# Part of the output stores issued by GpSimd, w_in loaded in three pieces, and the order table rearranged, in an attention and gated-convolution kernel on one core

## The chip, the cores and the metric

The kernel runs on one core of one Trainium2 chip. The metric is the time of one execution on the device, in microseconds (us). A run is called fast or slow by its agreement with the other runs of the same kernel, and only fast runs are compared. The engines are named as the profile names them: PE (matrix products), PEld (the loading of PE's weights), DVE (VectorE), ACT (ScalarE), POOL (GpSimd), SP (SyncE, which issues most DMAs). A profile has durations in ns where it gives the mean of one instruction, and in us elsewhere. The granted clock is the share of PE's full clock that the trace records as granted; where a trace has no clock record for a stretch, the views print 1.00.

## The reference, cut to what matters

```python
# q, k, v: [8 batches, 8 heads, 576, 64]; window of 32 to each side
scores = scale * q @ k^T
scores = where(|i - j| <= 32, scores, -1e9)
attn   = softmax(scores)
x      = (attn @ v) brought to [8, 576, 512]
# feed-forward part, d_ff = 1024, a convolution of 3 taps along the sequence
h      = relu(x @ w_in)
conv   = sum over k of conv_w[k] * h shifted by k - 1
out    = (h * sigmoid(conv)) @ w_out
```

## The kernel before

The kernel first makes a list of named operations (a cast, a product, a mask, a tap of the convolution, a store) and then emits them in the order of a long table. An entry such as `1047G1` reads: operation 1047, on GpSimd, with buffer 1. The letters are P (PE), V (VectorE), S (ScalarE), G (GpSimd), D (a DMA by SyncE), Q (a DMA issued by ScalarE); `2F` is two fillers, matmuls of a zero tile whose result nobody reads. Every engine works through its own entries in this order.

```python
BUFS = {'st': 3, 'qkb': 5, 'qkT': 3, 'attn': 2, 'rec': 4, 'xn': 3, 'hT0': 8, 'hT1': 6, 'hT2': 6, 'cp': 2, 'gT': 4, 'y': 7}
...
# a copy or cast on the engine that the table names
if e in loader:  loader[e].dma_start(out_, in_)
elif e == "S":   scalar.copy(out=out_, in_=in_)
elif e == "V":   vector.tensor_copy(out=out_, in_=in_)
else:            gpsimd.tensor_scalar(out=out_, in0=in_, scalar1=1.0, scalar2=0.0, op0=ALU.mult, op1=ALU.add)
...
# V shifted by half a block, for the odd blocks of queries
copy(e, vo[0:64, c0:c1], ve[64:128, c0:c1])
copy(e, vo[64:128, c0:c1], ve[0:64, c0 + 1:c1 + 1])
...
# the window's mask, after the exponential: both operands in SBUF
(vector if e_ == "V" else gpsimd).tensor_tensor(out=attn, in0=attn, in1=mask, op=ALU.mult)
...
# the convolution of one unit (128 channels x 384 positions); h is hT, in SBUF, pc is in PSUM
gpsimd.tensor_scalar(out=cp, in0=taps(kk), scalar1=w_tap(kk), scalar2=0.0, ...)      # a product on GpSimd
gpsimd.tensor_tensor(out=cp0, in0=cp0, in1=cp1, op=ALU.add)                          # their sum
tensor.matmul(pc, diag_w[:, kk, m, :], taps(kk), ...)                                # a tap on PE
vector.scalar_tensor_tensor(out=pc, in0=taps(kk), scalar=w_tap(kk), in1=from_, op0=ALU.mult, op1=ALU.add)
#   from_ is pc (PSUM) after taps on PE, or cp (SBUF) where GpSimd made the rest: a "lone tap"
vector.tensor_tensor(out=pc, in0=pc, in1=cp0, op=ALU.add)                            # PE's and GpSimd's parts
...
# stores: the table has D, SyncE, for all 36
loader[e_].dma_start(out_rows[r0:r0 + 128, :], y_sb.ap)
```

The gate, the eviction of q and k, xn and y read one operand from PSUM. The mask and the lone tap have two operands in SBUF. The casts and the shifts of V copy from SBUF to SBUF.

The softmax here doesn't subtract the row's maximum and nothing guards it: scores larger than these inputs give would overflow.

## Time and profile before

Before: 227.27 us, median of 3 runs (227.18 to 227.44). The profiled execution spans 225.6 us.

| engine | busy us | share of the span |
|---|---|---|
| PE | 211.5, of which 13.5 are fillers | 94% |
| VectorE | 197.3 | 87% |
| ScalarE | 187.5 | 83% |
| GpSimd | 137.7 | 61% |

The lines that carry the reading of the bound stand in the prediction. The following ones, from the groups of instructions of VectorE and GpSimd kept apart by shape, are the rows that the rest of this document is about. The columns are the source line, the engine, the operation, output and inputs, shapes and types, the count, then the busy time in us and the mean of one in ns, then the idle time before them and what ended it.

```profile
L232 DVE SCALAR_TENSOR_TENSOR gT<-pf,hT 128x384 bf16<-128x384 f32 x88 | 46.8, 548 | 5.4 <-ACT pf L232 5.1
...
L232 DVE TENSOR_TENSOR attn<-attn,mask 128x1152 bf16<-128x1152 bf16 x26 | 23.0, 886 | 2.4 <-ACT attn L232 2.3
L232 DVE SCALAR_TENSOR_TENSOR pf<-hT,conv_w_sb,cp 128x384 f32<-128x384 bf16 x33 | 20.4, 630 | 0.0
...
L232 DVE COPY vo<-ve 64x520 bf16<-64x520 bf16 x10 | 4.1, 410 | 0.7 <-ACT ve L232 0.5
```

```profile
L232 POOL TENSOR_TENSOR attn<-attn,mask 128x1152 bf16<-128x1152 bf16 x6 | 14.2, 2371 | 8.4 <-ACT attn L232 8.4
```

The gate reads PSUM and SBUF and takes 548 ns. The lone tap is of the same size, reads two tiles in SBUF, and takes 630 ns. The mask on GpSimd takes 2.4 us, more than two and a half times as long as on VectorE.

### The profile page before, as it was taken

To read this page: it belongs to the slowest core of one execution; us is meant where nothing else is said; L and a number is where in the kernel's file an instruction comes from. 1 tells how busy PE (TensorE), PEld (TensorE's weight loads), DVE (VectorE), ACT (ScalarE), POOL (GpSimd) and SP (SyncE) were. 2 spreads that over 40 slices of the span, in tenths; PEclk is the share of its full clock that TensorE was granted. 3 is DMA by queue.
4 is the path that set the end of the run, shared out by engine and by line. 5 is a ranking of instruction groups with operands and counts; after the bars stand their busy time and mean duration, and the time that the engine had idled before them with its cause. 6 is when DMAs were issued, how large, how long until landed. Compare 5 with 4: busy or idle time off the path is not lost.

```text
span 225.6 us, 7189 instructions
## 1 busy us (share of the span) xinstructions
PE 211.5 (94%) x2720; PEld 122.9 (54%) x2720; DVE 197.3 (87%) x467; ACT 187.5 (83%) x474; POOL 137.7 (61%) x203
## 2 busy tenths in 40 slices
PE   7698899989989999989999998999999999999993
PEld 5366567658555655545555454545655565455541
DVE  6279869899999979797999788989999999899990
ACT  2689899998989889879889989689989999777642
POOL 5978654654376937695368736756386735566640
PEclk9889999999999999999999999999999999999999
DMA  6999999999989999999997989994535212501224
GB/s 201 331 285 358 355 266 281 321 308 253 290 170 324 317 175 287 236 306 224 288 347 129 202 278 358 182 231 147 144 36 118 99 46 49 175 1 49 93 101 178
DMA packets 66391, 48.16 MB, mean 214 GB/s; under 512 B 50781, under 2 KB 50805, under 8 KB 66357
## 3 DMA queue, kind: packets, MB, share of 16 engines
q1 hardware_dynamic: 64992, 46.32, 78.6%
q10 hardware_dynamic: 1364, 1.39, 2.9%
q8 instruction: 21, 0.34, 0.8%
q14 instruction: 14, 0.11, 0.2%
HBM read 32.52 MB, written 9.44 MB: 186 GB/s over the span
## 4 chain that ended last, share of the span: by engine, by line
PE 41%; DVE 18%; ACT 17%; DMA 13%; issue 5%; SPq 3%; POOL 2%; DVEq 0%; ACTq 0%; POOLq 0%
PE pf L232 41%; DMA st<-in_k_dram 7%; ACT attn L232 6%; DVE pf L232 5%; DVE gT L232 4%; SPq L232 3%; DMA out_dram<-y 3%; ACT xn L232 3%; DVE qkT L232 2%; ACT pf L232 2%; DMA vo<-ve 2%; DVE attn L232 2%; DVE xn L232 2%; ACT qkb L232 2%; ACT y L232 1%
## 5 line engine op out<-in xcount | busy, mean ns | idle before, releaser
L232 PE MATMUL pf<-xT,w_in_sb 128*128 128x385 bf16 (+2 forms) x416 | 73.4, 315 | 3.6 <-ACT hT L232 0.9
L232 PE MATMUL pf<-w_out_sb,gT 128*128 128x512 bf16 x288 | 72.2, 380 | 0.0
L232 POOL TENSOR_SCALAR cp<-hT,conv_w_sb 128x384 f32<-128x384 bf16 (+1 forms) x63 | 38.9, 622 | 46.1 <-ACT hT L232 20.2
L232 ACT ACTIVATE pf<-pf 128x384 f32<-128x384 f32 (+1 forms) x104 | 48.2, 477 | 13.1 <-DVE pf L232 11.1
L232 DVE SCALAR_TENSOR_TENSOR gT<-pf,hT 128x384 bf16<-128x384 f32 (+1 forms) x104 | 52.1, 517 | 5.5 <-ACT pf L232 5.1
L232 PEld LDWEIGHTS <-w_in_sb 128*128 128x128 bf16 x416 | 38.6, 98 | 27.8 <-issue 4.5
L232 ACT ACTIVATE attn<-pf 128x512 bf16<-128x512 f32 (+1 forms) x96 | 41.4, 522 | 1.8 <-PE pf L232 1.8
L232 ACT ACTIVATE hT<-pf 128x385 bf16<-128x385 f32 (+2 forms) x76 | 35.4, 487 | 6.0 <-PE pf L232 5.6
L232 PEld LDWEIGHTS <-gT 128*128 128x128 bf16 x288 | 26.0, 98 | 25.7 <-DVE gT L232 0.5
L232 DVE SCALAR_TENSOR_TENSOR pf<-hT,conv_w_sb,pf 128x384 f32<-128x384 bf16 (+1 forms) x61 | 34.7, 586 | 1.2 <-PE pf L232 1.1
L232 PE MATMUL pf<-hT,diag_w 128*128 128x384 bf16 (+1 forms) x153 | 30.9, 309 | 0.9 <-DVE xn L232 0.6
L232 POOL TENSOR_SCALAR qkb<-st 128x1152 bf16<-128x1152 f32 (+1 forms) x23 | 25.7, 1122 | 7.6 <-DMA st<-in_k_dram 3.2
L232 DVE COPY qkT<-pf 128x576 bf16<-128x576 bf16 x35 | 25.6, 750 | 4.9 <-PE pf L232 4.9
L232 POOL TENSOR_TENSOR cp<-cp,cp 128x384 f32<-128x384 f32 (+1 forms) x24 | 24.4, 1016 | 1.6
L232 DVE TENSOR_TENSOR attn<-attn,mask 128x1152 bf16<-128x1152 bf16 x26 | 23.0, 886 | 2.4 <-ACT attn L232 2.3
L232 ACT ACTIVATE xn<-pf,rec 128x64 bf16<-128x64 f32 x96 | 22.0, 360 | 1.5 <-DVE rec L232 1.5
L232 ACT COPY y<-pf 128x512 f32<-128x512 f32 x30 | 18.1, 605 | 3.9 <-PE pf L232 3.7
L232 DVE SCALAR_TENSOR_TENSOR pf<-hT,conv_w_sb,cp 128x384 f32<-128x384 bf16 (+1 forms) x35 | 21.2, 618 | 0.0
L232 POOL TENSOR_TENSOR attn<-attn,mask 128x1152 bf16<-128x1152 bf16 x6 | 14.2, 2371 | 8.4 <-ACT attn L232 8.4
L232 DVE TENSOR_TENSOR xn<-pf,rec 128x256 bf16<-128x256 f32 x48 | 18.9, 410 | 0.0
L232 ACT COPY qkT<-pf 128x576 bf16<-128x576 bf16 x29 | 18.6, 664 | 0.4 <-PE pf L232 0.2
L232 PEld LDWEIGHTS <-diag_w 128*128 128x128 bf16 x153 | 13.3, 97 | 9.8 <-issue 1.3
(49 smaller groups left out, 235.2 us busy)
## 6 DMA issues: line engine op xcount, KB each, us to landing
st<-in_q_dram SPq DMA_DIRECT2D x16, 576.0 KB, 6.8
out_dram<-y SPq DMA_DIRECT2D x36, 256.0 KB, 3.8
st<-in_k_dram SPq DMA_DIRECT2D x14, 576.0 KB, 8.2
vst<-in_v_dram SPq DMA_DIRECT2D x24, 256.0 KB, 7.0
vst<-in_v_dram SPq DMA_DIRECT2D x15, 192.0 KB, 5.7
vo<-ve SPq DMA_DIRECT2D x11, 260.0 KB, 5.6
st<-in_moe_w_in_dram SPq DMA_DIRECT2D x2, 1024.0 KB, 9.3
st<-in_moe_w_out_dram SPq DMA_DIRECT2D x2, 1024.0 KB, 9.4
```

The source lines that it names most:

```text
L232: return lambda *args, **kwargs: fixed(do(*args, **kwargs))
```

## The change

The words that came with the change name the stores, w_in and the order. The diff holds more. Part of it, with cuts:

```diff
-BUFS = {'st': 3, 'qkb': 5, 'qkT': 3, 'attn': 2, 'rec': 4, 'xn': 3, 'hT0': 8, 'hT1': 6, 'hT2': 6, 'cp': 2, 'gT': 4, 'y': 7}
+BUFS = {'st': 4, 'qkb': 5, 'qkT': 3, 'attn': 2, 'rec': 7, 'xn': 2, 'hT0': 5, 'hT1': 8, 'hT2': 7, 'cp': 6, 'gT': 3, 'y': 5}
+MASKS = ('aa', 'mm', 'mm', 'mm', 'mm', 'mm', 'mm', 'mm')
 CONV = (
-    '33333333',
-    '33q3323r23223321',
+    '32r233q3',
+    'q2233r3q322q3321',
 ... (ten more rows; q, r: taps on GpSimd and a lone tap on VectorE)
 ORDER = """ ... every entry is new ... """
+    W_PARTS = {"in": ((0, 2), (2, 4), (4, MB)), "out": ((0, MB // 2), (MB // 2, MB))}
 ...
+                if added:      # the mask as a product on PE, ahead of the exponential: batch 0 only
+                    for n, e, width in ((2, x, 2), (0, 0, 8), (1, 1, 8)):
+                        tensor.matmul(ps[n]..., outside[rows, :], ident[rows, None, rows]..., start=True, stop=False)
 ...
-            loader[e_].dma_start(out_rows[r0:r0 + 128, :], y_sb.ap)
+            (gpsimd if e_ == "G" else loader[e_]).dma_start(out_rows[r0:r0 + 128, :], y_sb.ap)
```

Counted in the two built programs, from before to after: fillers 75 to 5; GpSimd's products for the convolution 63 to 78 and their sums 24 to 32; lone taps on VectorE 35 to 43; VectorE's taps on PSUM 61 to 38; VectorE's masks 26 to 19, GpSimd's 6 to 9, and batch 0's four on PE; q/k evictions on VectorE 35 to 24; shifts of V on VectorE 10 to 16 (nine of them of double width, which are two shifts in one instruction), on GpSimd 7 to 16, by DMA 11 to 8; stores by SyncE 36 to 21, by GpSimd 0 to 15. What it does in sum: work leaves ScalarE and VectorE for GpSimd, which had 39% of its time free.

## The prediction

> **What bounds the kernel now.** I read the page first, its busy shares and its chain of waits.
>
> ```profile
> PE 211.5 (94%) x2720; PEld 122.9 (54%) x2720; DVE 197.3 (87%) x467; ACT 187.5 (83%) x474; POOL 137.7 (61%) x203
> PE 41%; DVE 18%; ACT 17%; DMA 13%; issue 5%; SPq 3%; POOL 2%; DVEq 0%; ACTq 0%; POOLq 0%
> ```
>
> Three engines are nearly full and GpSimd (POOL) has room. The chain goes through PE, DVE and ACT in turn, so no single one is "the" bound. PE's 94% flatters it: ends of matmuls are modelled, and part of the work is not work. The list of groups kept apart by form shows the fillers, matmuls of zeros that only keep PE running:
>
> ```profile
> L232 PE MATMUL pf<-zero 128*128 128x256 bf16 x75 | 13.5, 330 | 1.3 <-DVE zero L232 1.3
> ```
>
> Without them PE has 211.5 - 13.5 = 198 us of busy time. Next, the table of busy time in four stretches that I chose: the head (until the first FFN matmul), the part in which attention and loads run beside the FFN, the dense part, and the end.
>
> ```profile
> core 0: us, PE busy (x) PEld busy (x) DVE busy (x) ACT busy (x) POOL busy (x), PEclk, DMA share, GB/s
> 0.00:26.00 26.00, 21.33 (x331) 14.66 (x332) 17.63 (x57) 18.73 (x46) 19.87 (x65) 0.93 0.98 299
> 26.00:136.00 110.00, 105.20 (x1560) 63.08 (x1559) 98.42 (x236) 99.09 (x253) 67.31 (x76) 1.00 1.08 267
> 136.00:191.00 55.00, 54.75 (x676) 30.14 (x676) 53.68 (x124) 48.73 (x131) 34.45 (x41) 1.00 0.58 139
> 191.00:226.00 35.00, 30.22 (x157) 15.03 (x155) 27.52 (x54) 20.97 (x46) 16.09 (x22) 0.98 0.28 98
> ```
>
> In the head PE is busy for 21.3 us, of which the same table for the zero tile alone gives 13.5 to the fillers: some 8 us of real work in 26. From 26 to 136, DVE and ACT each are busy for about 90%. From 136 to 191 DVE has 53.7 of 55 us: there PE and DVE are both full. The timeline tells where the head ends and what it waited for, and that ACT then ran without a break:
>
> ```profile
> 25.80 2.13 PE L232 MATMUL pf<-xT,w_in_sb 128*128 128x385 bf16 x12 [0.29 <-DVE xT L232]
> 6.26 0.72 ACT L232 CAST qkb<-st 128x640 bf16<-128x640 f32 x1 [3.52 <-DMA st<-in_q_dram]
> 16.40 3.11 ACT L232 ACTIVATE attn<-pf 128x128 bf16<-128x128 f32 x8
> ```
>
> Last, the waits of the queue that issues the DMAs: SyncE stands behind stores whose y is not yet made, and loads stand behind the stores.
>
> ```profile
> SPq L232 <- ACT y L232: 31.9, 13, 10.0
> ```
>
> The end is a copy of y after PE's last matmul (221.3 us) and a store (last issue 222.4, span 225.6), some 4.3 us.
>
> **What the Trainium skill says.** "TensorE: Matmul & The Clock Gate", Part 1 (the HAM clock gate): PE's clock is halved by default and released after about 3.4 us of activity. The trace agrees: granted clock 0.50 from 10 to 12 us, 0.72 from 12 to 14, 1.00 afterwards; the fillers are there for this. "DMA: Bandwidth & Descriptors", Issuing engines are not separate DMA queues: issuing from several engines saves only the sequencer's time to issue. The same page, SWDGE vs HWDGE vs iDMA: for a DMA from GpSimd a Q7 core computes the descriptors in software; before has no such DMA, so its trace can't say what that costs. "SBUF — State Buffer", Who interferes with whom: GpSimd shares a port pair with VectorE, and a VectorE instruction with two SBUF inputs contends with GpSimd's reads. The trace fits: the mask multiply takes 750 ns on DVE in the quiet head and 886 in the mean.
>
> **The change, part by part.** The built programs of both versions give the counts; the means are before's rows by form (busy over count).
>
> The title names stores, w_in and the order. The diff holds more: other pool sizes, other choices of the engine for conv taps, batch 0's mask added on PE before the exponential, V's shift more on DVE and GpSimd and less by DMA.
>
> PE: 70 of 75 fillers go, 70 x 0.18 = -12.6 us, nearly all in the head. Mask matmuls: 8 of 512 columns x 0.25 and 4 of 128 x 0.09 = +2.4. Transposes of x, 10 x 0.09 = -0.9. Conv taps: +6 x 0.225 - 6 x 0.126 = +0.6. Real work +2 us; busy about 201.
>
> DVE: taps onto PSUM -23 x 0.594 = -13.7; taps onto cp +6 x 0.618 + 2 x 0.4 = +4.5; q/k evictions -11 x 0.731 = -8.0; masks -7 x 0.885 = -6.2; q/k casts (two each of 512, 640 and 1152 columns, from 0.43 us for 512, scaled: an estimate) +3.8; V shifts +9 of double width (estimate 0.8) - 3 x 0.41 = +6.0; y +4 x 0.68 = +2.7; xn +6 x 0.394 = +2.4; diagonals +9 x 0.19 (from a copy of that size) = +1.7; other casts about -0.5. Sum -7.3: about 190.
>
> ACT: q/k casts -5 x 1.17 - 3 x 0.72 = -8.0; xn -24 x 0.229 = -5.5; q/k evictions +11 x 0.641 = +7.1; y -4 x 0.603 = -2.4; other casts -2 x 0.63 - 3 x 0.62 - 0.7 = -3.8; xT -1.6. Sum -14.2: about 173.
>
> POOL: cp products +11 x 0.617 + 4 x 0.63 = +9.3; cp sums +6 x 1.03 + 2 x 0.59 = +7.4; masks +3 x 2.37 = +7.1; V shifts (7 of double width, estimate 1.4; 3 x 0.69; one of 1.9 gone) = +10; casts about +7.7; diagonals -9 x 0.37 = -3.3; constants for the mask +1.2. Sum +39: about 177. Then 15 stores; at an estimated 1 us of descriptor work each (from the first-byte latency that "DMA: Bandwidth & Descriptors", Specifications, gives for that path) 15 us more, so 192 of some 221.
>
> So the change empties ACT and DVE into GpSimd. What that is worth, stretch by stretch:
>
> Head: ahead of the first FFN matmul the order has 5 fewer casts, one eviction and 8 fewer xn multiplies on ACT: 5 x 0.7 + 0.64 + 1.84 - 0.65 (one more xT) = 5.3 us less in a run that lasts from 6.3 to 25.6 us; on DVE 4 masks and 2 xT copies less (4.4 us), some casts and multiplies more. Against it, the first k now is third behind two q loads: 1.7 MB instead of 1.35 MB, at some 0.33 MB/us about 1 us later. And PE is cold without fillers, about 1 us. 5.3 - 2 = 3.3; I take 3.5 for some DVE relief.
>
> Middle and dense part: summing the same means between milestones of the order, DVE saves nothing until the first pair of batches is through (it has more shifts there), then about 5 us in the second pair, 1 in the third and 3 in the last. ACT saves about 9 by the end of the first pair (5 of them the head's), 6 in the second, then nothing. DVE's savings fall where it is 90 to 98% busy, but PE is as full there and does not get less work. I give half of 9: 4.5.
>
> Given back: GpSimd at 80 to 87% makes cp later and holds the shared port longer: +1 to +2 us. Stores on GpSimd free SyncE for loads, but DMA is far from its limit after 136 us and prefetched before: +-0. The end keeps its y copy and store: 0. w_in in three loads is inside the head.
>
> Sum: 227.3 - 3.5 - 4.5 + 1.5 = 220.8.
>
> **The rivals.** (1) PE is the bound: then its full stretches from 136 to 221 do not shrink and only the head counts, 227.3 - 3.5 = 224, within 2%. For it: 54.75 of 55 us. Against: a contiguous run of 31 matmuls of 512 columns took 7.00 us, 0.226 each, while their group averages 380 ns each; some of the "busy" is the drain of a matmul that another engine holds up. (2) GpSimd becomes the bound or a late link: tap waits for cp, PE and tanh for tap. For it: +54 us on an engine whose operations take twice as long (mask 2371 against 886 ns), with in-order stores that wait for y. Then 226 to 230. Against: in before GpSimd mostly waited for others (20.2 us on hT from ACT, 17.0 on DVE), and cp now has six buffers in place of two, so it may run ahead. (3) The order was made for the new counts and the stalls shrink more than in proportion: DVE at the same share of the span, 190 / 0.874 = 217.
>
> **Range and chances.** Between rivals 3 and 2 I set 215.5 to 226.5 for 8 in 10. The line of 2% faster is at 222.7; my figure lies 2 us below it, with an uncertainty of some 4 us: about two in three for faster. Over 231.8 needs rival 2 at its worst.
>
> **What the profile after should show.** The first FFN matmul at 21 to 23.5 us in place of 25.8; granted clock well under 1 beyond 14 us; DVE 187 to 194 us busy, ACT 170 to 177, POOL 170 to 185, PE near 200; SyncE's wait on y below 25 us; the end still about 4 us. The prediction is wrong if the head is not shorter, if DVE or PE wait for cp for more than a few us in total (before: 0.7), or if DVE's rows of two SBUF inputs grow by over 5%.

## The result and the profile after

After: 250.94 us, median of 4 runs (250.09 to 252.00); before, in the same rounds, 227.36 us (227.18 to 230.82). The ratio is 1.104, with a 95% interval of 1.098 to 1.111. Ratios in this document are the mean time of one kernel's fast runs over that of the other's of the same rounds, so they are not quite the ratio of the medians. The change made the kernel 23.6 us slower, and the prediction of 220.8 us was wrong in its sign.

First the busy shares and the chain of waits of the page after:

```profile
PE 208.9 (83%) x2627; PEld 121.2 (48%) x2652; DVE 219.9 (88%) x463; ACT 176.3 (70%) x440; POOL 190.7 (76%) x258
DVE 40%; PE 32%; issue 12%; POOL 5%; ACT 4%; DMA 4%; SPq 1%; POOLq 0%; DVEq 0%; ACTq 0%
```

In the chain VectorE has gone from 18% to 40%. It has less work than before by count of instructions (463 in place of 467) and yet 22.6 us more of busy time. The groups kept apart by shape, VectorE first and then GpSimd, show where it is:

```profile
L233 DVE SCALAR_TENSOR_TENSOR gT<-pf,hT 128x384 bf16<-128x384 f32 x88 | 45.6, 547 | 2.6 <-ACT pf L233 2.0
L233 DVE SCALAR_TENSOR_TENSOR pf<-hT,conv_w_sb,cp 128x384 f32<-128x384 bf16 x39 | 33.9, 881 | 1.7 <-POOL cp L233 0.6 <-PE pf L233 0.3
L233 DVE TENSOR_TENSOR attn<-attn,mask 128x1152 bf16<-128x1152 bf16 x19 | 22.5, 1183 | 0.2 <-ACT attn L233 0.2
...
L233 DVE COPY vo<-ve 64x1040 bf16<-64x1040 bf16 x9 | 10.2, 1139 | 0.3
...
L233 DVE COPY vo<-ve 64x520 bf16<-64x520 bf16 x7 | 4.8, 679 | 2.1 <-POOL ve L233 2.0
```

```profile
L233 POOL TENSOR_TENSOR attn<-attn,mask 128x1152 bf16<-128x1152 bf16 x9 | 22.1, 2451 | 4.2 <-ACT attn L233 4.0
...
L233 POOL DMA_DIRECT2D out_dram<-y x15 | 8.9, 593 | 4.8 <-ACT y L233 4.8
```

The gate, with one operand in PSUM, is at 547 ns as before. The lone tap went from 630 to 881 ns, the mask from 886 to 1183, the single shift of V from 410 to 679, and the double shift takes 1139 ns. The rows of VectorE that grew all read two operands in SBUF, or copy, cast or scale from SBUF to SBUF. The 15 stores cost GpSimd 8.9 us. The waits tell who stood behind VectorE; first two lines of before, then the same two of after:

```profile
ACT pf L232 <- DVE pf L232: 11.1, 18, 1.2
...
PE pf L232 <- DVE gT L232: 1.3, 3, 0.6
```

```profile
ACT pf L233 <- DVE pf L233: 25.0, 28, 3.2
...
PE pf L233 <- DVE gT L233: 10.8, 15, 2.4
```

ScalarE's tanh waited 11.1 us for VectorE's taps and now waits 25.0. PE waited 1.3 us for gates and now 10.8; by shape, 3.8 us of that stand before products of q and k and 4.0 before taps, and only 0.3 before the last product, so it is not only the gate's result that PE wants (what else it wants there, a free PSUM bank for one, is not shown). The timeline shows one such place. The columns are the start and the duration in us:

```profile
46.88 0.32 DVE L233 COPY vo<-ve 64x520 bf16<-64x520 bf16 x1
...
47.85 2.36 POOL L233 TENSOR_TENSOR attn<-attn,mask 128x1152 bf16<-128x1152 bf16 x1
...
48.09 2.27 DVE L233 COPY vo<-ve 64x520 bf16<-64x520 bf16 x1
...
51.23 0.32 ACT L233 ACTIVATE pf<-pf 128x192 f32<-128x192 f32 x1 [3.19 <-DVE pf L233]
```

The shift of V that takes 0.32 us at 46.88 takes 2.27 us at 48.09. It began 0.24 us after a mask on GpSimd and ended 0.15 us after that mask. The tap behind it came late, and ScalarE stood for 3.19 us. There was a second cost, which the table of stretches shows (its length, then busy time and count of PE, PEld, DVE, ACT and POOL, then PE's granted clock, the DMA share and GB/s):

```profile
48.00:50.00 2.00, 1.19 (x8) 0.41 (x6) 1.97 (x2) 0.04 (x1) 2.00 (x1) 1.00 0.00 1
50.00:52.00 2.00, 0.52 (x14) 0.43 (x15) 1.97 (x6) 0.78 (x3) 1.83 (x4) 0.70 0.00 0
52.00:54.00 2.00, 1.67 (x26) 1.20 (x23) 1.78 (x7) 0.75 (x5) 1.08 (x3) 0.50 0.04 9
...
58.00:60.00 2.00, 2.00 (x34) 1.29 (x32) 2.00 (x4) 1.53 (x3) 1.90 (x3) 1.00 1.14 335
```

PE had little to do from 48 to 52 us, and from 50.8 to 57.6 us it was granted half of its clock; after a pause of 2.4 us it was again at half from 102.0 to 105.4. Before has its clock at 1.00 from 26 to 191 us. The clock is not where most of the loss lies: after's two fast runs with a mean clock of 0.977 and 0.978 took 1.6 us more than the two with 0.990 and 0.991.

To see whether that one place is the rule, I sorted VectorE's instruction records by whether a GpSimd instruction was running at their start. Count and mean in ns:

```
                          before, beside / alone     after, beside / alone
lone tap 128x384             7, 682 / 26, 616          37, 895 /  2, 620
mask 128x1152               12, 1045 / 14, 750         14, 1339 / 5, 748
gate 128x384 (PSUM)         no difference              no difference
```

The undisturbed lengths are the same in both kernels. What changed is how often the two engines meet, and how much is lost when they do. Summed over the rows that work from SBUF alone, the excess over each shape's shortest tenth is about 6 us before and 33 us after (18 in run 11 and 6 in run 8 below); over all other rows together it is about 5 us in both.

The records show more than a correlation. Of the 35 lone taps of 384 columns that began beside a GpSimd instruction other than a store, 29 ended 405 to 425 ns after that instruction's end, however long it still took. The longest:

```profile
201.22 2.37 POOL L233 TENSOR_TENSOR attn<-attn,mask 128x1152 bf16<-128x1152 bf16 x1 [1.13 <-ACT attn L233]
...
202.07 1.94 DVE L233 SCALAR_TENSOR_TENSOR pf<-hT,conv_w_sb,cp 128x384 f32<-128x384 bf16 x1
```

This tap began 1.52 us before the mask ended and ended 0.42 us after it. So the tap is held until GpSimd's instruction is done. Whether that carries the 23.6 us is for the experiments.

Where the time went, by the start of the first FFN matmul of each of the four pairs of batches and the start of the last matmul (us; the cuts are good to half a us, and after's trace lacks 25 of the 288 matmuls of the last product):

| | head | pair 0 | pair 1 | pair 2 | pair 3 | end |
|---|---|---|---|---|---|---|
| before | 25.8 | 54.3 | 51.7 | 47.3 | 42.2 | 4.3 |
| after | 27.4 | 63.6 | 53.2 | 54.0 | 46.4 | 5.7 |

The lines of after that answer to the other ones shown in the prediction: the fillers, the first FFN matmul as the chain has it, two of its stretches (pairs 0 and 2), and SyncE's first wait.

```profile
L233 PE MATMUL pf<-zero 128*128 128x256 bf16 x5 | 1.2, 316 | 0.0
```

```profile
27.38 1.75 PE pf L233 x10
```

```profile
27.40:91.00 63.60, 54.17 (x810) 34.74 (x816) 59.78 (x132) 47.66 (x126) 53.89 (x68) 0.95 0.82 223
...
144.20:198.20 54.00, 48.80 (x568) 27.07 (x569) 51.80 (x101) 42.27 (x101) 47.19 (x56) 1.00 0.44 114
```

```profile
SPq L233 <- ACT y L233: 24.3, 4, 11.0
```

Pair 0 lasts 63.6 us, of which VectorE is busy for 59.8 and PE for 54.2; pair 2 lasts 54.0, with 51.8 and 48.8. PE, which was as full as VectorE before, now has gaps, and VectorE is the fullest engine in both.

### The profile page after: what moved, and what is told of

It is laid out like the page before. It is cut to its first block, busy times and chain, and to the rows that moved or that the text cites. A ratio compares the mean times of both kernels' runs of the same rounds, so it can differ in the third digit from the quotient of the medians.

```text
span 250.3 us, 7023 instructions
## 1 busy us (share of the span) xinstructions
PE 208.9 (83%) x2627; PEld 121.2 (48%) x2652; DVE 219.9 (88%) x463; ACT 176.3 (70%) x440; POOL 190.7 (76%) x258
## 4 chain that ended last, share of the span: by engine, by line
DVE 40%; PE 32%; issue 12%; POOL 5%; ACT 4%; DMA 4%; SPq 1%; POOLq 0%; DVEq 0%; ACTq 0%
PE pf L233 32%; DVE pf L233 12%; DVE gT L233 9%; DVE vo L233 4%; DMA st<-in_k_dram 4%; DVE attn L233 4%; POOL cp L233 3%; ACT attn L233 2%; DVE xn L233 2%; DVE hT L233 2%; DVE qkT L233 2%; DVE ve L233 1%; DVE rec L233 1%; SPq L233 1%; POOL vo L233 1%
## 5 line engine op out<-in xcount | busy, mean ns | idle before, releaser
L233 POOL TENSOR_SCALAR cp<-hT,conv_w_sb 128x384 f32<-128x384 bf16 (+1 forms) x78 | 53.7, 697 | 24.0 <-ACT hT L233 15.2
L233 PEld LDWEIGHTS <-gT 128*128 128x128 bf16 x288 | 26.4, 99 | 29.1 <-DVE gT L233 1.9
L233 DVE SCALAR_TENSOR_TENSOR pf<-hT,conv_w_sb,cp 128x384 f32<-128x384 bf16 (+1 forms) x43 | 37.8, 890 | 1.7 <-POOL cp L233 0.6
L233 POOL TENSOR_SCALAR qkb<-st 128x1152 bf16<-128x1152 f32 (+2 forms) x26 | 30.2, 1166 | 6.6 <-PE pf L233 3.8
L233 POOL TENSOR_TENSOR cp<-cp,cp 128x384 f32<-128x384 f32 (+1 forms) x32 | 33.7, 1056 | 1.2
L233 POOL TENSOR_TENSOR attn<-attn,mask 128x1152 bf16<-128x1152 bf16 x9 | 22.1, 2451 | 4.2 <-ACT attn L233 4.0
L233 PE MATMUL pf<-ident,qkb 64*128 64x64 bf16 x576 | 14.6, 196 | 10.5 <-DVE qkb L233 6.4
L233 DVE SCALAR_TENSOR_TENSOR pf<-hT,conv_w_sb,pf 128x384 f32<-128x384 bf16 (+1 forms) x38 | 21.5, 571 | 1.6 <-PE pf L233 0.8
L233 DVE COPY qkT<-pf 128x576 bf16<-128x576 bf16 x24 | 17.4, 747 | 6.0 <-PE pf L233 5.4
L233 DVE TENSOR_TENSOR attn<-attn,mask 128x1152 bf16<-128x1152 bf16 x19 | 22.5, 1183 | 0.2 <-ACT attn L233 0.2
L233 PE MATMUL pf<-qkT 64*128 64x64 bf16 x576 | 15.9, 197 | 8.0 <-DVE gT L233 3.8
L233 PE MATMUL pf<-ve,attn 128*64 128x65 bf16 x320 | 16.8, 207 | 6.1 <-DVE y L233 1.5
```

Source lines behind the costliest of these rows:

```text
L233: return lambda *args, **kwargs: fixed(do(*args, **kwargs))
```

## The experiments

Two theories stand against each other. The **port theory**: VectorE's instructions with two SBUF operands, and its copies within SBUF, are slowed or stopped by GpSimd's reading, and the new order makes them meet. The **order theory**: the new order has stalls of its own (late links, a slow head, stores), and the slow rows are beside the point. Each kernel below was run with the kernel before on the same chip; the ratio is to before's fast runs. After itself is at 1.104. Differences in us from after are between medians; the runs were not all on one chip, and by the ratios the gain of run 11, the one that differs most of those used below, is 15.2 us and not 13.3.

**1. The stores back to SyncE.**

```diff
-429G 437G 433G ... (15 entries)
+429D 437D 433D ...
```

> The changed kernel with its 15 GpSimd stores issued by SyncE again, at the same places of the order. The stores are 15 of 0.593 us = 8.9 us of GpSimd's 190.7 busy. Port theory (VectorE waits while GpSimd holds the port that they share): GpSimd has some 9 us less, so VectorE's busy time falls from 219.9 by 0 to 3 us and the time from 250.9 by 0 to 4. Store theory (descriptors made in software, in-order stores that hold GpSimd up, are the cause of the loss): the time falls by 12 us or more. If SyncE's loads get stuck behind the stores: slower than 251.

Measured: 253.15 us (252.98 to 253.38), ratio 1.114 (1.106 to 1.122). GpSimd's 8.9 us are gone and nothing was gained. The stores in the change's title are not the cause; VectorE's 219.2 us and its lone tap at 887 ns are as in after.

**2. Only the buffers: before with four cp in place of two.**

```diff
-'cp': 2, 'gT': 4, 'y': 7}
+'cp': 4, 'gT': 4, 'y': 6}      # and the zero tile 256 wide, to make room
```

> The kernel before with 4 cp buffers in place of 2 (to make room y has 6 in place of 7 and the zero tile is half as long); order, engines and counts are as before. With 2 buffers GpSimd stood still for 17.0 us until VectorE had read cp; 4 take this wait away. Port theory: GpSimd now works while VectorE reads cp, so the tap on cp (630 ns in the mean, 7 of 33 begun while GpSimd ran) grows to 700 to 880 ns, VectorE's busy time from 197.3 by 3 to 9 us, and the time from 227.3 to 229 to 236, although only a wait was removed. Order theory (the loss is waits that the new order makes): a wait fewer, 224 to 227.5, the tap on cp unchanged.

Measured: 227.85 us (226.80 to 229.98), ratio 1.004 (0.995 to 1.014). The wait of GpSimd for VectorE to free a cp, 17.0 us before, is gone, and its wait for hT from ScalarE took the place:

```profile
POOL cp L232 <- ACT hT L232: 20.2, 10, 4.1
POOL cp L232 <- DVE pf L232: 17.0, 15, 4.2
```

```profile
POOL cp L230 <- ACT hT L230: 26.9, 15, 6.0
```

The lone tap is at 648 ns. More buffers alone do not bring the engines together, so my guess that they did falls, and with it what the port theory had forecast for this run (229 to 236 us).

**3. The lone tap with one SBUF operand**. Its output is wrong, which doesn't matter for the time.

```diff
+                if from_ is not pc:
+                    vector.tensor_scalar(out=pc, in0=taps(kk), scalar1=w_tap(kk), scalar2=0.0, op0=ALU.mult, op1=ALU.add)
+                    return
```

> The changed kernel with the 43 taps on cp reading hT alone (a product, not product plus cp): wrong results on purpose. Same count of VectorE instructions of 384 columns, same order, GpSimd's work the same; they read one SBUF operand and so should not need the shared port. Port theory: these rows fall from 881 to 550 to 640 ns, VectorE's busy time from 219.9 to 205 to 212, the time by 6 to 14 us to 237 to 245. Order theory: VectorE and PE wait for each other as before, the time falls by less than 4 us. (VectorE no longer waits for cp either; that was 0.6 us.)

Measured: 241.24 us (240.47 to 243.35), ratio 1.064 (1.055 to 1.072); VectorE 203.8 us busy in place of 219.9. With GpSimd running beside it as before, the row is at its undisturbed length:

```profile
L231 DVE TENSOR_SCALAR pf<-hT,conv_w_sb 128x384 f32<-128x384 bf16 x39 | 23.6, 613 | 1.3 <-ACT qkT L231 0.5 <-PE pf L231 0.3 <-ACT hT L231 0.2
```

One operand less, 43 instructions of the same size at the same places: 9.7 us back. The operation has another name now, but that is not it: the taps that take their sum from PSUM keep the old one and are at 614 ns in after. The instruction no longer waits for cp either, which run 15 below separates.

**4. The head's loads in before's order** (first q, k, q, k, then v, then w_in).

> The changed kernel with its first loads in another order: q, k, q, k of batch 0, then v, then the first part of w_in, in place of q, q, k, v, w_in, k, v. Head theory: the second k lands about 3 us earlier (it was 13.3 us), the first FFN matmul comes 1 to 3 us before 27.4, and the end moves by as much if the head is part of the loss: 248 to 250. Port theory says nothing of the head; it expects that most of the 23.6 us stays: above 246.

Measured: 252.65 us (252.41 to 252.91), ratio 1.112 (1.106 to 1.119). The first FFN matmul comes at 28.1 us, not earlier. The order of loads is not the loss.

**5. All masks on PE**, as the change does for batch 0.

```diff
-MASKS = ('aa', 'mm', 'mm', 'mm', 'mm', 'mm', 'mm', 'mm')
+MASKS = ('aa', 'aa', 'aa', 'aa', 'aa', 'aa', 'aa', 'aa')   # the 28 mask entries dropped
```

> The changed kernel with the mask added by PE ahead of the exponential in all batches, as it does already for batch 0 (results stay right). VectorE's 19 mask multiplies (22.5 us, of which 8 are their slowing beside GpSimd) and GpSimd's 9 (22 us) go; PE gets 28 x 0.46 = 13 us more. Port theory: GpSimd at some 168 us reads less, the taps on cp fall from 881 towards 800 ns, the copies too; VectorE 190 to 196 us busy and 235 to 245 us in all. Order theory (the new order itself makes the engines wait for one another, the slow rows are beside the point): PE is as full as before and gets more, so 250 to 258 us.

Measured: 237.94 us (236.93 to 239.27), ratio 1.044 (1.036 to 1.052). VectorE 187.8, GpSimd 163.3, PE 209.4 us busy. The double shift of V fell to 502 ns, although nothing of it was touched. The gain was as the port theory forecast.

**6. VectorE's copies on ScalarE.**

```diff
-20V1 26V3 25V 29V ... (31 entries)
+20S1 26S3 25S 29S ...
```

> The changed kernel with VectorE's copies from SBUF to SBUF (16 shifts of V, 6 casts of v, 6 of q and k, 3 of w_out) on ScalarE, which is 70% busy (results stay right). Port theory: VectorE loses some 28 us of busy time, 12 of them slowing, and ScalarE gets about 20, each copy at its own undisturbed length; 243 to 248 us. Order theory: the work only moves between two engines that have the same links in the chain: 249 to 256 us. If ScalarE's copies are slowed beside GpSimd as VectorE's are (over 1.0 us for the double width), the port theory is wrong about who shares.

Measured: 253.52 us (251.59 to 256.42), ratio 1.105 (1.094 to 1.116); its profile fell in a slow run. VectorE fell to 196.9 us, ScalarE rose from 176.3 to 198.3, and nothing was gained: a miss of the port theory's figure. The first FFN matmul comes at 32.7 us in place of 27.4, since ScalarE's casts now stand in the head's chain, and behind the head only 1 us is won in this slow run (216.1 us to the last matmul, against 217.3). ScalarE stands in this run's chain with 22% and VectorE with 21%, so that 22 us more on ScalarE undo the relief is the likely reason, but no run shows it. One thing is plain all the same: the nine double shifts take 1056 or 1057 ns on ScalarE, all of them, beside the same GpSimd. The expectation had taken a length over 1.0 us for slowing; it is ScalarE's own length.

**7. Runs 3, 5 and 6 together** (wrong result).

> The changed kernel with all three at once: a tap alone reads hT only (wrong result on purpose), masks on PE, copies on ScalarE. No VectorE instruction of any weight then has two SBUF inputs or copies SBUF to SBUF. Port theory: the loss is gone, 222 to 233 us, VectorE below 175 us busy. Order theory: still 238 us or more, since the order is the same.

Measured: 244.20 us (243.59 to 245.04), ratio 1.071 (1.064 to 1.079), a result that looks like the order theory's. One line of the waits tells why it is not a fair test:

```profile
PE pf L230 <- ACT qkb L230: 10.5, 1, 10.5
```

PE stood 10.5 us for a single cast of q or k that I had moved to ScalarE, and ScalarE is at 198.7 us. I had given the chain a new link. So runs 3 and 5 were joined without it.

**8. Runs 3 and 5 together** (wrong result).

> The changed kernel with a tap alone reading hT only (wrong result on purpose) and the mask on PE in all batches; the copies stay on VectorE, since moving them to ScalarE made the head 5 us later and so hid what it was to show. What is left of the slowing is under 4 us. Port theory: both savings add, 250.9 - 9.7 - 13 = 228, and 13 us more of PE hold some of it back: 226 to 233 us, VectorE about 178 us busy. Order theory: what is left after either of them is the order's own stalls, so the two together save hardly more than one: 235 us or more.

Measured: 232.23 us (231.29 to 232.69), ratio 1.019 (1.013 to 1.025); VectorE 181.0, PE 207.2 us busy, granted clock 1.00. The two savings add: 18.7 us of the 23.6 are gone. Of the stretches, head and end stay long (28.1 and 5.3 us), and the four pairs take 56.3, 49.0, 49.1 and 43.2 us, in sum 197.6 against 195.5 before and 217.2 after. What is left there of the new order's cost is about 2 us.

**9. The head's V work on ScalarE**, six entries of GpSimd.

> The changed kernel with the head's six V operations of GpSimd (four shifts, two casts) on ScalarE, which is busy for 14 of the head's 27 us there. The chain of waits of the head goes through them from 19 to 24 us. If they are why the head is not shorter: first FFN matmul at 24 to 26 us in place of 27.4, and 1.5 to 4 us off the time. If the late k (landed at 13.3 us) alone is why: 27 us or later and no gain.

Measured: 253.58 us (253.00 to 254.99), ratio 1.114 (1.106 to 1.122); the first FFN matmul at 29.4 us. A miss; that ScalarE has these copies in front of the exponentials, which then come later, is a guess.

**10. A candidate: before with GpSimd's six masks on PE.**

> A candidate that could beat both: the kernel before with GpSimd's six masks (2.4 us each, during which a VectorE copy or tap can stand still) added on PE (6 x 0.46 = 2.8 us more there), order unchanged, results right. Port theory: VectorE's masks and copies get shorter by 1 to 3 us in sum and GpSimd 14 us emptier, so cp comes earlier: 224 to 228 us. If PE is the bound: 228 to 231 us.

Measured: 228.25 us (226.91 to 230.29), ratio 1.003 (0.995 to 1.010). VectorE's mask went from 886 to 859 ns, but its lone tap went from 630 to 660 and its busy time from 197.3 to 198.7, where the port theory wanted 1 to 3 us less. It does not beat before.

**11. In after, only GpSimd's nine masks on PE.** VectorE keeps its 19 and every other instruction.

```diff
+ON_PE = [(1, 1, 1), (2, 1, 1), (3, 1, 0), (4, 0, 0), (4, 1, 0), (5, 1, 0), (6, 0, 0), (6, 1, 0), (7, 0, 1)]
+                added = added or (b, i, x) in ON_PE
+                if (b, i, x) in ON_PE:     # in the mask's own emission
+                    return
```

> The changed kernel with only GpSimd's nine masks added on PE (9 x 0.46 = 4 us more there); VectorE keeps its 19 masks and all its work. Port theory: the 2.45 us instructions beside which a VectorE copy stands still are gone; VectorE's busy time falls by 7 to 13 us without an instruction less, and the time by 4 to 10 us, to 241 to 247. If the gain of the run with all masks on PE came from VectorE's 19 multiplies being taken away: VectorE's busy time within 4 us of 219.9 and the time 249 to 253 us.

Measured: 237.66 us (237.20 to 239.97), ratio 1.037 (1.023 to 1.052), as much as with all masks on PE. The busy line, and VectorE's mask and double shift:

```profile
PE 206.3 (88%) x2654; PEld 120.4 (51%) x2679; DVE 203.2 (86%) x463; ACT 176.9 (75%) x440; POOL 167.0 (71%) x249
```

```profile
L232 DVE TENSOR_TENSOR attn<-attn,mask 128x1152 bf16<-128x1152 bf16 x19 | 17.2, 907 | 0.2 <-ACT attn L232 0.2
...
L232 DVE COPY vo<-ve 64x1040 bf16<-64x1040 bf16 x9 | 6.2, 684 | 0.3
```

VectorE executes the same 463 instructions in 203.2 us in place of 219.9: 16.7 us less without an instruction less. Its mask went from 1183 to 907 ns, the double shift from 1139 to 684. This is more than the port theory had forecast (241 to 247 us). PE's clock stays at 1.00, which may be part of the gain. A rival is that GpSimd, with 22 us less to do, is merely less late. The waits speak against it: PE and VectorE stood behind GpSimd for 6.2 us in all in after and for 5.5 here.

**12. In after, GpSimd's nine masks on VectorE**, the fuller engine.

```diff
-196G 1047G 1142G ... (9 entries)
+196V 1047V 1142V ...
```

> The changed kernel with GpSimd's nine masks on VectorE, the engine that is already fuller: nine instructions more there (9 x 0.75 = 7 us at the undisturbed length), 22 us less on GpSimd. Port theory: the copies' slowing (9 to 11 us) goes with them, so VectorE's busy time is 214 to 222 us in spite of the nine more, and the time 245 to 251 us. Load theory (what counts is how much work VectorE has): VectorE 226 to 230 us busy and 255 to 260 us.

Measured: 247.27 us (242.84 to 248.97). Two of the four runs are slow ones, the profiled one among them; the fast ones are 242.84 and 246.26 us, with a ratio of 1.064 (1.041 to 1.088). From the profile, of a slow run, only the work of VectorE is read:

```profile
PE 209.2 (85%) x2627; PEld 121.0 (49%) x2652; DVE 213.4 (86%) x472; ACT 177.2 (72%) x440; POOL 170.3 (69%) x249
```

```profile
L231 DVE TENSOR_TENSOR attn<-attn,mask 128x1152 bf16<-128x1152 bf16 x28 | 27.0, 973 | 0.2 <-ACT attn L231 0.2
```

VectorE has nine masks more than in after and is busy for 6.5 us less, and all four runs are below after's fastest, 250.09 us. The load theory, which wanted 255 us or more, is refuted.

**13. The control: before with the masks of batches 1 to 7 on PE.**

> Control for the runs with masks on PE: the kernel before with the masks of batches 1 to 7 on PE (28 x 0.46 = 13 us more there, VectorE 20 us and GpSimd 14 us less), order unchanged, results right. If the gain of 13 us in the changed kernel came from the masks' work as such, before gains too: 216 to 222 us, a version that beats both. If it came from the slowing, which before has little of: 226 to 233 us, since PE was full already.

Measured: 234.16 us (232.92 to 235.21), ratio 1.019 (1.009 to 1.029). The move that gives after 13 us makes before slower, by about 2%: PE is at 217.5 us there, and VectorE, at 183.9, waits for PE for some 20 us. So the gain in after is not the masks' work as such.

**14. A right result without the costly meetings**: run 11, and each lone tap as a PE matmul of the centre tap and a VectorE sum of PSUM and cp.

```diff
+                if from_ is not pc:
+                    tensor.matmul(pc.ap[:, 0:nc_], diag_w[:, kk, m, :], taps(kk), start=True, stop=True)
+                    vector.tensor_tensor(out=in3(pc.ap), in0=in3(pc.ap), in1=in3(from_.ap), op=ALU.add)
+                    return
```

> The changed kernel with a right result and without the two costly meetings: GpSimd's nine masks on PE (+4 us there), and each of the 43 lone taps as one PE matmul of the centre tap (43 x 0.17 = +7 us) and a VectorE sum of PSUM and cp, which has one SBUF operand (557 ns in both traces so far, whatever GpSimd does). Port theory: VectorE falls from 203 to some 188 us, the sum's row stays under 570 ns, and the time comes near the run with both savings: 230 to 238 us. If the taps' saving there came only from not waiting for cp, nothing is gained over 237.7: 237 us or more, with VectorE waiting for cp or PE.

Measured: 270.57 us (268.41 to 271.91), ratio 1.187 (1.174 to 1.200), the worst of all.

```profile
L232 DVE TENSOR_TENSOR pf<-pf,cp 128x384 f32<-128x384 f32 x42 | 23.4, 564 | 42.5 <-PE pf L232 37.8 <-POOL cp L232 2.4 <-POOL qkb L232 1.9
```

The sum is at 564 ns, undisturbed as expected, but VectorE waited 37.8 us for PE before it. The matmul stands in PE's queue at the place of VectorE's tap, and PE, which works in order, reaches it late. The forecast of 230 to 238 us failed. The run says what the place in the order is worth, and nothing about the second operand.

**15. The lone tap reading cp and not hT** (wrong result): one SBUF operand, and the wait for GpSimd's product stays.

```diff
-                        out=pc, in0=taps(kk), scalar1=w_tap(kk), ...      # run 3
+                        out=pc, in0=cp, scalar1=w_tap(kk), ...
```

> The changed kernel with the lone tap reading cp only and not hT (wrong result on purpose): one SBUF operand as in the run that read hT only, but it still waits for GpSimd's product. If the second SBUF operand cost the 10 us: the tap's row at 600 to 630 ns and 238 to 244 us. If the dropped wait for cp gave them: VectorE waits for cp by 5 us or more in sum and the time is 247 us or more.

Measured: 242.47 us (241.44 to 243.42), ratio 1.067 (1.061 to 1.074). The row:

```profile
L231 DVE TENSOR_SCALAR pf<-cp,conv_w_sb 128x384 f32<-128x384 f32 x39 | 23.5, 614 | 1.8 <-POOL cp L231 0.6 <-PE pf L231 0.3 <-ACT hT L231 0.2
```

It is at 614 ns and waited 0.6 us for cp in all. Of run 3's 9.7 us, 8.5 are still gained: it is the second operand, not the dependency, that costs them.

**16 and 17. Dose and control on before.** Two idle operations of GpSimd after a finished cp: reading SBUF, or only writing it. By an oversight they were emitted only after the sums of two products, so 48 in place of 78, and some 30 us of GpSimd in place of 48.

```diff
+            def extra():
+                for _ in range(2):
+                    gpsimd.tensor_scalar(out=scratch[:, 0:384], in0=mask[..., 0:384], ...)   # 16
+                    gpsimd.memset(scratch, 0.0)                                              # 17
```

> The kernel before, unchanged in its order, with two idle operations of GpSimd after each finished cp that read a constant tile in SBUF (128x384 each, about 0.6 us; 78 in all, about +48 us of GpSimd, 186 in all, as in the changed kernel). Results stay right. Port theory: VectorE's taps on cp, 630 ns, rise above 720 and the masks above 950, VectorE's busy time rises by 6 to 14 us and the time by 5 to 14. If the loss is due to the order and not to GpSimd's company: taps below 660 ns, time within 3 us of before, apart from what a later cp costs, which the next run shows too.

> The control: the same places and about the same busy time of GpSimd, but the two idle operations only write SBUF (memsets of 128x640) and read nothing. Port theory, if it is GpSimd's reading that counts: taps on cp below 670 ns, and only the copies suffer; VectorE's busy time within 4 us of before and the time within 4 us. If any work of GpSimd slows VectorE, or if a later cp is what costs: the same time as the run with reads, within 2 us.

Measured: with reads 233.96 us (233.62 to 235.52), ratio 1.026 (1.020 to 1.032); with writes 233.65 us (232.06 to 234.64), ratio 1.024 (1.017 to 1.031). The lone taps, with reads and then with writes:

```profile
L232 DVE SCALAR_TENSOR_TENSOR pf<-hT,conv_w_sb,cp 128x384 f32<-128x384 bf16 x33 | 23.8, 725 | 5.0 <-POOL cp L232 4.8
```

```profile
L232 DVE SCALAR_TENSOR_TENSOR pf<-hT,conv_w_sb,cp 128x384 f32<-128x384 bf16 x33 | 21.6, 660 | 4.8 <-POOL cp L232 4.8
```

The lone taps follow the port theory: 725 ns with reads, 660 with writes, 630 before. The rest missed its figures: the masks with reads are at 901 ns (over 950 expected), VectorE's busy time is 201.5 and 197.6 us (4 us more with reads, 6 to 14 expected), and with writes the time was to stay within 4 us of before. The times do not tell the two apart: VectorE waits 4.8 us for a later cp in both. For the time, this pair is inconclusive, and by the words of the second expectation it speaks for the later cp. Instruction by instruction it is clear: in the run with writes, 13 lone taps met a memset and nothing else of GpSimd, and took 619 ns (627 at most; 614 for the six that met nothing); in the run with reads, 11 met an added read and nothing else, and took 711 (860 at most). A GpSimd instruction that only writes did not hold the lone tap.

## Why the prediction was wrong

**The step that failed** is "the means are before's rows by form", in the working for VectorE. The prediction read that GpSimd shares a port pair with VectorE, cited 750 against 886 ns for it, and then took 886 and 618 ns over into a kernel with 54 us more of GpSimd's work, with "+1 to +2 us" for the whole effect in "Given back". The counts were right and the durations were not. VectorE was to fall by 7.3 us to 190 and came to 219.9. Of the 29.9 us between, 39 lone taps at 881 in place of 618 ns make 10.3, the four short ones 2.3, 19 masks at 1183 in place of 885 make 5.7, nine double shifts at 1139 in place of the estimated 800 make 3.1, the seven single ones 1.9, six casts of v 2.2, nine diagonals 1.4: 26.9 us, all in rows that read and write within SBUF or read two tiles there. (The working also forgot to take off the one q/k cast that VectorE had before, 0.4 us, which changes nothing.) The estimate of 0.8 us for the double shift was itself too high for a free VectorE, where it takes 426 ns, so the slowing of that row is even larger than the miss.

What the runs showed in its place: runs 3 and 15 that the lone taps' second SBUF operand costs 8 to 10 us; run 11 that GpSimd's nine masks cost 13 us, and run 12 that they do it by what they do to VectorE, since VectorE gets faster even when it takes them over; run 8 that the two add to 18.7 of 23.6 us (13 us more on PE, and VectorE's own masks gone, are in that run too, so it is not a pure measure). The Trainium skill has the mechanism ("SBUF — State Buffer", Who interferes with whom): an instruction in a two-port mode and GpSimd exclude each other for a whole instruction, and one with two SBUF inputs contends with GpSimd's reads; ScalarE waits for neither. The trace agrees with all three (that the shift of V is in such a mode is inferred from its stop): a shift of 0.32 us stood until GpSimd's mask was done, 2.27 us; ScalarE's nine double shifts took the same 1057 ns (run 6); a lone tap took 895 ns beside GpSimd and 620 alone, and ended about 0.41 us after GpSimd's instruction did; the gate, with one SBUF operand, took 547 ns in either case.

**The head** was to be 3.5 us shorter and was 1.6 us longer. ScalarE's savings were counted right (13.8 us busy in place of 18.5), but they were not on the path. In the chain of waits of after, the head goes through the last load of k (landed at 13.3 us, 9.35 us after its issue), then through a cast on VectorE, 2.1 us of PE and ScalarE, and from 19 to 24 us through GpSimd's shifts and casts of V. Neither the loads' order (run 4) nor ScalarE for the V work (run 9) made it shorter. What would is left open. On the clock the prediction was right, although the views print 1.00 for the whole head: after's trace has its first clock record at 26.9 us. The spacing of matmuls tells what came earlier. The transposes of x, 128x128, follow each other at 107 ns in after, from 24.6 to 26.4 us, and at 56 ns in before, at 22.8 us; fillers come at 213 ns in after at 26.6 us, and in before at 213 ns up to 6.2 us and at 109 from 13.9 us. So without fillers PE ran the end of the head at half its pace, and since no change of the clock is on record before 26.9 us, presumably all of it. PE has 2.5 us of the head's chain before the first FFN matmul, so this cost 1.3 us at most (an estimate: half of them); how much of the 1.6 us it is, no run shows. (The prediction's reading of before's clock left out that it was granted at 1.00 from 6.3 to 9.7 us, before it fell to 0.50.)

**The middle** was to gain 4.5 us and lost 21.7: pairs 0 to 3 took 217.2 us in place of 195.5. With the meetings gone (run 8) they take 197.6 us, so the 4.5 us are not there even then.

**The rest of the steps.** ScalarE: 173 predicted, 176.3 measured. GpSimd: 177 and 15 for the stores, 190.7 measured; the stores cost 593 ns each and not 1 us, and the rest took 4.8 us more than predicted: GpSimd's own rows grew too (its product went from 622 to 699 ns). SyncE's wait for y fell from 31.9 to 24.3 us, below the 25 predicted, and it was worth nothing, as predicted. PE: 201 predicted and 208.9 measured; its busy time includes the drain of matmuls that others hold up. The end was to stay at 4.3 us and is 5.7; putting the stores back (run 1) did not shorten it (6.0), and its cause is open.

**The rivals.** The first rival (PE alone) is refuted by VectorE's 40% of the chain. The second was the right engine and the wrong way: GpSimd did not become a late link, VectorE waits for cp for 0.6 us; it reached the path through the company it keeps. The prediction had argued against it that cp "may run ahead"; running ahead is what brings the two engines together. The third put the span at VectorE's busy time over 0.874: with the measured 219.9 that is 251.6, against a span of 250.3. It fits here, though not in the runs with masks on PE (187.8 us in a span of 234.9), so it is no rule. The prediction had named "VectorE's rows of two SBUF inputs grow by over 5%" as a sign that it was wrong; they grew by 40% and 34%, and it gave this far too little room in the range.

**What stays open**: the head's 1.6 us and the end's 1.4, and the share of the 18.7 us that run 8 owes to masks taken off VectorE rather than to the slowing. No run beat before. The best form of the new order with a right result is run 11, 237.66 us.

## What to carry to other kernels

Before moving work to GpSimd, list VectorE's instructions that have two operands in SBUF or copy within SBUF, and ask how many will run beside GpSimd; a duration read in a profile holds only for the company it was measured in. Long GpSimd instructions are the ones to move first (nine masks of 2.45 us cost some 13 us here): a copy of 0.3 us stood behind a whole one, and what waited for VectorE stood too. Test with a run in which GpSimd's work is given to the busier engine: if that gets faster, it is the company that costs.

## What the Trainium skill lacked or had wrong

- "SBUF — State Buffer", Who interferes with whom, says that a VectorE instruction with two SBUF inputs contends with GpSimd's reads and that the second of the two is blocked until the first is done, but not how long the blocked one still needs then. Here it was less than its whole length: a lone tap of 0.62 us ended 405 to 425 ns after GpSimd's instruction in 29 of 35 cases. The means, 895 ns in place of 620 for a lone tap begun beside GpSimd (of 37) and 1339 in place of 748 for a mask (of 14), with 2970 at most, are this kernel's own.
- "DMA: Bandwidth & Descriptors", Specifications, gives about 1 us to the first byte for a DMA issued by GpSimd, from which the prediction took GpSimd's own cost. What a store occupies GpSimd with is 593 ns here (mean of 15), and the page has no figure for it.
- "TensorE: Matmul & The Clock Gate", Part 1, ties the halved clock to an idle window of about 3.4 us. Here the clock fell to 0.50 at 50.8 us, when PE had been busy for 1.75 of the last 3.40 us and the longest gap in its records had been 1.07 us (matmul records can be missing, but the weight loads show the same gap), and at 102.0 us, 2.3 us into a pause. So shorter pauses were enough. The page tells of clocks that oscillate with such pauses, without a figure for how short they may be.
